# RetNet attention and squared-ReLU FFN on one core: the first block's weight conversion split over three engines, with a third staging buffer and reordered loads

## Chip, cores and metric

One core of a Trainium2 chip runs the whole program. The metric is the device time of one execution in microseconds. The kernel before took 1168.56 us (median of 3 runs, 1168.07 to 1169.2).

## What is computed

The reference, cut to what matters: retention with a decay mask for 8 batches of 8 heads (576 positions, head size 64), and on its output, as 4608 tokens of width 512, two matrix products with a squared ReLU between them (d_ff = 2048). q, k and v are float32; the two weights arrive as float64.

```python
scores = q @ k.T / sqrt(64)                     # per batch and head, 576 x 576
ret = scores * where(rel >= 0, gamma[h] ** rel, 0)
x = (ret @ v).transpose(0, 2, 1, 3).reshape(4608, 512)
h = maximum(x @ w_in, 0.0)                      # w_in 512 x 2048
out = (h * h) @ w_out                           # w_out 2048 x 512
```

## The kernel before

**Attention.** Each batch is cut into chunks of 128 positions (the fifth of a batch has 64), 40 chunks in all. In iteration i of the main loop the kernel runs `retain(i-2)` (L247: the output of a chunk and the running state), `scores(i-1)` (L227) and `turn(i)` (L214: transposes of q and k), and starts the loads of chunk i+2. q, k and v of a full chunk are 256 KB each, loaded by SP's queue at L123. TensorE, VectorE (DVE), ScalarE (ACT), GpSimd (POOL) and SP each work through their own queue in program order. `scores` writes two PSUM banks from the pool `ps_a` (three banks, shared with the transposes and the output of `retain`); VectorE frees them with the masking at L240, which writes `ret`. POOL makes `vs` at L244, from v and the decay `dv`. `qT` is multiplied by the decay `dq` at L223; ScalarE copies kT (L225), the output xT (L272) and the state u (L285). `dq` is 1152 KB and is loaded in one piece behind q, k and v of chunk 0 (L188), `dv` (20 KB) behind it.

**FFN.** Tokens go in 9 blocks of 512. After each of the three parts of an iteration `ffn()` (L474) lets as many steps of the current block run as the tokens done have earned; so TensorE's order of steps is fixed when the program is built. Blocks 1 to 8 use a scheme of seven products (`ffn_in`, `ffn_out`), which needs sums of weight blocks. Block 0 uses the plain products instead: 16 steps `first_in` (L290, eight 128x512 matmuls L297, ReLU on ScalarE L299 into a buffer `r`, square on VectorE L300), then 8 steps `first_out` (L314, sixteen matmuls L322 into four banks `acc`). Beside them the weights are converted and the sums for blocks 1 to 8 are made: `sum_w_in` (L302, four POOL passes per step), and in `first_out` four POOL passes (L328 to L331) over the staging buffer of w_out, after which SP writes its seven parts to DRAM (`w2_dram`, L332, 896 KB). From there blocks 1 to 8 fetch them (L420, 1 MB each).

**Conversion.** The weights are cut into 32 pieces of 512 KB float64 (16 of w_in, then 16 of w_out). `fetch_w` (L146) loads a piece as raw 8-byte words into one of four places in the tiles G that block 0 leaves free. `round_w` (L152) makes float32 of it with five VectorE and two POOL passes of 128x512, in which VectorE waits for POOL in the middle:

```python
nc.vector.tensor_scalar(exp, hi, 20, 0x7FF, ...)                 # L165
nc.gpsimd.tensor_scalar(exp, exp, 1151.0, 896.0, ...)            # L166
nc.gpsimd.tensor_scalar(exp, exp, -896.0, 2.0 ** 23, ...)        # L168
nc.vector.tensor_scalar(bits, hi, 0xFFFFF, 0x100000, ...)        # L170
nc.vector.scalar_tensor_tensor(t, lo, 2.0 ** -32, bits, ...)     # L171
nc.vector.scalar_tensor_tensor(t, t, 2.0 ** -20, exp, ...)       # L172
nc.vector.scalar_tensor_tensor(bits, hi, 0x80000000, bits, ...)  # L173
```

`prepare` (L175) fetches piece j+2 and converts piece j. It is called after each part of every iteration until the 16 pieces of w_in are done (14 of them before the first `first_in`), and then before the steps of block 0. A w_in piece goes straight to `wa` or `wb`; two w_out pieces share a staging buffer `w_stage`, of which there are two (pool `w2_pool`). The results of a block go out through two tiles `o0` and `o1` of `o_pool`.

Of the kernel before, what the change touches and what calls it, by code (L numbers as in the profile page):

```python
# [37 lines left out]
def kernel(  # L38
# [66 lines left out]
    W2_SLOT = {n: j for j, n in enumerate(("B11", "T3", "B21", "B22", "T1", "T2", "T4"))}  # L105
# [4 lines left out]
    exp_room = [G[3][:, 4 + j, :, :].rearrange("p a b -> p (a b)") for j in range(2)]  # L110
# [41 lines left out]
    def round_w(j):  # L152

        t = piece_dst(j)
        if piece_src(j).dtype == F32:
            nc.sync.dma_start(t.rearrange("p (c f) -> p c f", c=N_DM), piece_src(j))
            return  # L160
        words = raw_room[j % 4].bitcast(U32).rearrange("p (n two) -> p n two", two=2)
# [24 lines left out]
    load(0)
    dq = const.tile([128, HP, S], F32, name="dq")
    nc.sync.dma_start(dq, decay_q)  # L188
    dv = const.tile([128, H, NCH], F32, name="dv")
    nc.sync.dma_start(dv, decay_v)  # L190
# [36 lines left out]
    def scores(i):  # L227
# [3 lines left out]
        sc = [ps_a.tile([128, HP, C], F32, tag="a", name=f"sc{e}") for e in range(2)]  # L231
# [82 lines left out]
    def first_out(m):  # L314

        assert 2 * N_M + 2 * m + 1 < n_ready[0]
# [13 lines left out]
        nc.gpsimd.tensor_tensor(t4, b21, t2, op=ALU.subtract)  # L330
        nc.gpsimd.tensor_tensor(b12, b22, b12, op=ALU.subtract)  # L331
        nc.sync.dma_start(w2_dram[:, :, m, :].rearrange("o p d -> p o d"), s[:, 0:7, :])  # L332
        if m == N_M - 1:
            for half in range(2):
                o = o_pool.tile([128, 2, d_model], F32, tag=f"o{half}", name=f"o{half}")
                for j in range(2):
                    (nc.vector.tensor_copy if j else nc.scalar.copy)(o[:, j, :], acc[2 * half + j])
                store(0, half, o)
# [85 lines left out]
    def ffn_out(n, j, tt):  # L424
# [14 lines left out]
        if j == 0:  # L439
            for half in range(2):  # L440
                o_t[half] = o_pool.tile([128, 2, d_model], F32, tag=f"o{half}", name=f"o{half}")
        c11, c12 = o_t[0][:, :, 0:HT], o_t[0][:, :, HT:]
        c21, c22 = o_t[1][:, :, 0:HT], o_t[1][:, :, HT:]
# [113 lines left out]
```

## Time and profile before

| | |
|---|---|
| median of 3 runs | 1168.56 us |
| profiled execution | 1167.34 us |
| its span | 1165.6 us |
| mean granted TensorE clock | 0.971 |
| TensorE busy | 1081.1 us (93%) |
| VectorE, POOL, ScalarE busy | 416.7, 387.3, 146.2 us |
| first matmul of `first_in` | at 66.04 us |
| first matmul of `ffn_in` (block 1) | at 251.10 us |

Times in the rows below are counted from the start of the span. A busy time is the sum of an engine's instructions. The granted clock is that of TensorE as a share of full speed. Behind an arrow stands what ended the idle time before an instruction.

### The profile page before, as it was taken

What the parts mean: (1) busy time and instruction counts of PE and PEld (TensorE: products, weight loads), DVE (VectorE), ACT (ScalarE), POOL (GpSimd) and SP (SyncE); (2) the same over time, 40 slices, a digit from 0 to 9 for tenths busy, and PEclk for the clock granted to TensorE, in tenths of its full rate; (3) what the DMA queues carried; (4) which work ended last, traced back from release to release, by engine and by line L of the source; (5) the groups of instructions that cost most, each with busy time, mean ns of one, the idle gap of its engine ahead of it and who ended that gap; (6) DMA issues with size and microseconds to landing.
All of it is one profiled execution on the core that took longest, in us unless ns stands there. A gap on an engine that the chain in (4) does not pass through costs nothing.

```text
span 1165.6 us, 15121 instructions
## 1 busy us (share of the span) xinstructions
PE 1081.1 (93%) x6464; PEld 881.0 (76%) x6464; DVE 416.7 (36%) x610; ACT 146.2 (13%) x287; POOL 387.3 (33%) x372
## 2 busy tenths in 40 slices
PE   3496987679999999999999999999999999999998
PEld 2353543258888888888888888888888888888886
DVE  4886244544412531243125312431253134302410
ACT  1111200011110111111111111111111011100100
POOL 2443046574502440244024402440244024402520
PEclk9788997789999999999999999999999999999999
DMA  9673043355056114701451146015511550033032
GB/s 257 163 173 91 1 128 128 108 142 153 5 172 190 28 35 134 209 19 29 155 181 37 46 136 195 19 38 162 168 27 55 157 165 1 37 116 138 1 109 109
DMA packets 141571, 122.77 MB, mean 105 GB/s; under 512 B 114496, under 2 KB 129856, under 8 KB 134208
## 3 DMA queue, kind: packets, MB, share of 16 engines
q1 hardware_dynamic: 138912, 112.36, 33.8%
q0 software_dynamic: 2592, 9.44, 2.0%
q8 instruction: 51, 0.84, 0.3%
q14 instruction: 16, 0.13, 0.0%
HBM read 105.01 MB, written 16.78 MB: 104 GB/s over the span
## 4 chain that ended last, share of the span: by engine, by line
PE 79%; POOL 7%; DVE 6%; issue 4%; DMA 3%; SPq 1%; POOLq 0%; DVEq 0%
PE h_b L381 14%; PE o_b L431 13%; PE h_c L381 9%; PE h_a L381 9%; PE o_a L431 9%; PE o_c L431 8%; PE h_ps L297 3%; PE sc L235 3%; PE x_ps L262 3%; PE x_ps L258 2%; DMA w_dram<-w_stage 2%; POOL g L168 2%; POOL g L166 2%; PE acc_ps L322 1%; PE kT_ps L220 1%
## 5 line engine op out<-in xcount | busy, mean ns | idle before, releaser
L431 PE MATMUL o_b<-w,g 128*128 128x256 f32 x768 | 172.5, 381 | 0.0
L431 PEld LDWEIGHTS o_b<-w,g 128*128 128x128 f32 x768 | 144.5, 190 | 19.9
L381 PE MATMUL h_a<-xT,wa 128*128 128x256 f32 x512 | 122.5, 382 | 0.0
L431 PE MATMUL o_c<-w,g 128*128 128x256 f32 x512 | 115.4, 381 | 0.0
L431 PE MATMUL o_a<-w,g 128*128 128x256 f32 x512 | 114.9, 381 | 0.0
L431 PEld LDWEIGHTS o_c<-w,g 128*128 128x128 f32 x512 | 96.2, 190 | 13.6
L431 PEld LDWEIGHTS o_a<-w,g 128*128 128x128 f32 x512 | 96.3, 190 | 13.3
L381 PEld LDWEIGHTS h_a<-xT,wa 128*128 128x128 f32 x512 | 95.8, 190 | 13.7
L322 PE MATMUL acc_ps<-w_stage,g 128*128 128x512 f32 x128 | 67.6, 688 | 30.1 <-DVE w_stage L173 30.1
L408 POOL TENSOR_TENSOR g<-g 128x512 f32<-128x512 f32 x32 | 40.6, 1269 | 118.7 <-DVE g L389 115.4
L322 PEld LDWEIGHTS acc_ps<-w_stage,g 128*128 128x128 f32 x128 | 27.9, 224 | 65.5 <-issue 33.1
L389 DVE SCALAR_TENSOR_TENSOR g<-g 128x512 f32<-128x512 f32 x96 | 75.4, 786 | 3.3
L244 POOL TENSOR_TENSOR vs<-v_ld,dv 128x512 f32<-128x512 f32 (+1 forms) x40 | 42.2, 1055 | 98.8 <-issue 80.6
L400 POOL TENSOR_TENSOR g<-g 128x512 f32<-128x512 f32 x32 | 33.2, 1037 | 119.1 <-ACT g L399 114.7
L342 POOL DMA_DIRECT2D out_dram<-o x18 | 13.5, 748 | 176.7 <-issue 56.1
L240 DVE TENSOR_TENSOR ret<-sc,msk 128x512 f32<-128x512 f32 (+1 forms) x80 | 47.1, 628 | 60.7 <-PE sc L235 60.7
L381 PE MATMUL h_b<-xs,ws 128*128 128x256 f32 x256 | 60.9, 381 | 0.5 <-DVE xs L354 0.5
L381 PE MATMUL h_b<-xT,wb 128*128 128x256 f32 x256 | 60.9, 381 | 0.3 <-POOL xT L355 0.3
L381 PE MATMUL h_c<-xT,ws 128*128 128x256 f32 x256 | 61.0, 381 | 0.0
L381 PE MATMUL h_b<-xs,wb 128*128 128x256 f32 x256 | 61.0, 381 | 0.0
L381 PE MATMUL h_c<-xs,ws 128*128 128x256 f32 x256 | 60.9, 381 | 0.0
L220 PE MATMUL kT_ps<-ident,k_ld 128*128 128x128 f32 (+1 forms) x160 | 25.4, 286 | 36.8 <-DVE ret L240 36.6
(84 smaller groups left out, 1402.1 us busy)
## 6 DMA issues: line engine op xcount, KB each, us to landing
w<-w_dram SPq DMA_DIRECT2D x56, 1024.0 KB, 5.0
out_dram<-o POOLq DMA_DIRECT2D x18, 512.0 KB, 6.0
q_ld<-in_q_dram SPq DMA_DIRECT2D x32, 256.0 KB, 5.9
k_ld<-in_k_dram SPq DMA_DIRECT2D x32, 256.0 KB, 6.5
v_ld<-in_v_dram SPq DMA_DIRECT2D x32, 256.0 KB, 4.3
g<-in_moe_w_in_dram SPq DMA_DIRECT2D x16, 512.0 KB, 4.2
g<-in_moe_w_out_dram SPq DMA_DIRECT2D x16, 512.0 KB, 5.7
w_dram<-w_stage SPq DMA_DIRECT2D x8, 896.0 KB, 4.9
```

What stands on the lines that cost most here:

```text
L220: nc.tensor.transpose(p[:, hp, :cs], loaded[i][j][:cs, 2 * hp:2 * hp + 2, :], ident[:cs, :cs])
L235: nc.tensor.matmul(sc[e][:cs, hp, :cs], lhsT=kT[sl, hp, :cs], rhs=qT[sl, hp, :cs], start=True, stop=True)
L240: nc.vector.tensor_tensor(r[:cs, :, :cs], sc[e][:cs, :, :cs], msk[:cs, :, :cs].to_broadcast([cs, HP, cs]), op=ALU.mult)
L244: nc.gpsimd.tensor_tensor(vs[:cs], loaded[i][2][:cs], dv[:cs, :, ci:ci + 1].to_broadcast([cs, H, D]), op=ALU.mult)
L262: nc.tensor.matmul(p[half, hp, :cs], lhsT=s["vs"][:cs, 2 * hp + e, :], rhs=s["ret"][e][:cs, hp, :cs], start=(ci == 0 and hp == 0), stop=Tr ...
L297: nc.tensor.matmul(p, lhsT=w[:, cc, :], rhs=xT[0][:, cc, :], start=(cc == 0), stop=(cc == N_DM - 1))
L322: nc.tensor.matmul(acc[ts], lhsT=g0(m + e * N_M)[:, ts * 128:(ts + 1) * 128], rhs=s[:, 2 * e:2 * e + 2, :].rearrange("p a b -> p (a b)"), ...
L381: nc.tensor.matmul(p[:, mm, :], lhsT=w[:, c, :], rhs=xs[n][right][:, c, :], start=(j in OPENS and mm == 0 and c == 0), stop=(j in CLOSES a ...
L389: nc.vector.scalar_tensor_tensor(t, t, 0.0, t, op0=ALU.max, op1=ALU.mult)
L400: nc.gpsimd.tensor_tensor(g["A11"], g["A11"], g["A11"], op=ALU.mult)
L408: nc.gpsimd.tensor_tensor(g["S3"], g["A11"], g["S1"], op=ALU.subtract)
L431: nc.tensor.matmul(p[:, tt, :], lhsT=G[m // 2][:, G_SLOT[left], m % 2, tt * 128:(tt + 1) * 128], rhs=w2[j][:, m, :], start=(j in OPENS and ...
```

## The change

The conversion of a piece becomes three functions. `round_a` has two VectorE passes (exponent, mantissa bits) and three new ScalarE passes: the low word scaled to float32 and written back in place, the exponent clamped and shifted by a Relu with a bias, and the sign as +1 or -1 over the high word. `round_b` multiplies exponent and sign on POOL. `round_c` adds the two parts of the mantissa and multiplies by the scale, on VectorE. `prepare` issues `round_a` and `round_b` of piece j and then `round_c` of piece j-1, so the stages of two pieces overlap; after it, piece j+4 is fetched, into one of five places instead of four. The first five pieces are fetched together in iteration 1, behind the loads of chunk 3. `prepare` no longer runs in iterations 0 to 2 but from iteration 3 to 5 (three times each), and then before the steps of block 0 as before, up to two pieces further ahead.

For w_out there are three staging buffers in turn (the third is the tile of `o_pool`, which becomes one tile for both halves of an output block). The four sums are made on VectorE as soon as both pieces are converted (`sum_w_out`), instead of on POOL in `first_out`, and the writes to DRAM (`keep_w_out`, now two DMAs) are issued when the next buffer's first piece is done. The square in `first_in` goes from VectorE to POOL, in place, without the buffer `r`. The scores of chunks 0 to 3 use the banks of `ps_f` instead of `ps_a`. Of `dq`, the first 128 columns are loaded right behind q of chunk 0, `dv` behind k, and the rest behind v.

The diff's core (the order of the parts in `w2_dram`, the assertions and the indexing of `o` are left out):

```diff
-    g_room = [G[2][:, 2 + j:4 + j, :, :] for j in (0, 2)] + [G[3][:, j:j + 2, :, :] for j in (0, 2)]
+    g_room = [G[2][:, 2 + j:4 + j, :, :] for j in (0, 2)] + [G[3][:, j:j + 2, :, :] for j in (0, 2, 4)]
...
+            if i == 0 and name == "q":
+                nc.sync.dma_start(dq[:, :, 0:C], decay_q[:, :, 0:C])
+            if i == 0 and name == "k":
+                nc.sync.dma_start(dv, decay_v)
+        if i == 0:
+            nc.sync.dma_start(dq[:, :, C:], decay_q[:, :, C:])
...
-            stage[m] = w2_pool.tile([128, N_M, d_model // 2], F32, tag="w2", name="w2_stage")
+            pool, tag = (o_pool, "o") if m % 3 == 2 else (w2_pool, "w2")
+            stage[m] = pool.tile([128, 8, d_model // 2], F32, tag=tag, name="w2_stage")
...
+    def round_a(j):
+        t = halves[j] = piece_dst(j)
+        words = raw_room[j % N_RAW].bitcast(U32).rearrange("p (n two) -> p n two", two=2)
+        f32s = raw_room[j % N_RAW].rearrange("p (n two) -> p n two", two=2)
         lo, hi = words[:, :, 0], words[:, :, 1]
-        bits = t.bitcast(U32)
         exp = exp_room[j % 2].bitcast(U32)
         nc.vector.tensor_scalar(exp, hi, 20, 0x7FF, op0=ALU.logical_shift_right, op1=ALU.bitwise_and)
-        nc.gpsimd.tensor_scalar(exp, exp, 1151.0, 896.0, op0=ALU.min, op1=ALU.max)
-        nc.gpsimd.tensor_scalar(exp, exp, -896.0, 2.0 ** 23, op0=ALU.add, op1=ALU.mult)
-        nc.vector.tensor_scalar(bits, hi, 0xFFFFF, 0x100000, op0=ALU.bitwise_and, op1=ALU.bitwise_or)
-        nc.vector.scalar_tensor_tensor(t, lo, 2.0 ** -32, bits, op0=ALU.mult, op1=ALU.add)
-        nc.vector.scalar_tensor_tensor(t, t, 2.0 ** -20, exp.bitcast(F32), op0=ALU.mult, op1=ALU.mult)
-        nc.vector.scalar_tensor_tensor(bits, hi, 0x80000000, bits, op0=ALU.bitwise_and, op1=ALU.bitwise_or)
+        nc.vector.tensor_scalar(t.bitcast(U32), hi, 0xFFFFF, 0x100000, op0=ALU.bitwise_and, op1=ALU.bitwise_or)
+        nc.scalar.activation(f32s[:, :, 0], lo, AF.Copy, scale=2.0 ** -32)
+        nc.scalar.activation(exp, exp, AF.Relu, bias=exp_bias[:, 0:1], scale=2.0 ** 23)
+        nc.scalar.activation(f32s[:, :, 1], hi, AF.Sign, bias=exp_bias[:, 1:2], scale=-1.0)
+    def round_b(j):
...
+        nc.gpsimd.tensor_tensor(exp_room[j % 2], exp_room[j % 2], f32s[:, :, 1], op=ALU.mult)
+    def round_c(j):
...
+        nc.vector.tensor_tensor(t, f32s[:, :, 0], t.bitcast(U32), op=ALU.add)
+        nc.vector.scalar_tensor_tensor(t, t, 2.0 ** -20, exp_room[j % 2], op0=ALU.mult, op1=ALU.mult)
+    def sum_w_out(m):
+        b11, b12, b21, b22, t1, t2, t4, t3 = (stage[m][:, j, :] for j in range(8))
+        nc.vector.tensor_tensor(t1, b12, b11, op=ALU.subtract)
+        nc.vector.tensor_tensor(t3, b22, b12, op=ALU.subtract)
+        nc.vector.tensor_tensor(t2, b22, t1, op=ALU.subtract)
+        nc.vector.tensor_tensor(t4, b21, t2, op=ALU.subtract)
+    def keep_w_out(m):
+        nc.sync.dma_start(w2_dram[0, :, m, :], stage[m][:, 0, :])
+        nc.sync.dma_start(w2_dram[1:7, :, m, :].rearrange("o p d -> p o d"), stage[m][:, 2:8, :])
+    def prepare():
+        j = n_made[0]
...
+                round_a(j)
+                round_b(j)
...
+        j -= 1
+        if j >= 0:
+            if wide:
+                round_c(j)
+                fetch_w(j + N_RAW)
+            wi, m, e = pieces[j]
+            if wi == 1 and m > 0 and e == 0:
+                keep_w_out(m - 1)
+            if wi == 1 and e == 1:
+                sum_w_out(m)
+                if m == N_M - 1:
+                    keep_w_out(m)
...
-        sc = [ps_a.tile([128, HP, C], F32, tag="a", name=f"sc{e}") for e in range(2)]
+        pool, tag = (ps_f, "f") if i < TOK // C else (ps_a, "a")
+        sc = [pool.tile([128, HP, C], F32, tag=tag, name=f"sc{e}") for e in range(2)]
...
-        r = work2.tile([128, TOK], F32, tag="qT", name="r")
+        r = g0(m + e * N_M)
         nc.scalar.activation(r, p, AF.Relu)
-        nc.vector.tensor_tensor(g0(m + e * N_M), r, r, op=ALU.mult)
+        nc.gpsimd.tensor_tensor(r, r, r, op=ALU.mult)
...
-        nc.gpsimd.tensor_tensor(t1, b12, b11, op=ALU.subtract)
-        nc.gpsimd.tensor_tensor(t2, b22, t1, op=ALU.subtract)
-        nc.gpsimd.tensor_tensor(t4, b21, t2, op=ALU.subtract)
-        nc.gpsimd.tensor_tensor(b12, b22, b12, op=ALU.subtract)
-        nc.sync.dma_start(w2_dram[:, :, m, :].rearrange("o p d -> p o d"), s[:, 0:7, :])
...
+                if n_made[0] <= 2 * N_M + 5 + (2 * args[0] if f == first_out else 0):
+                    prepare()
...
+    def early(i):
+        if TOK // C - 1 <= i <= TOK // C + 1:
+            prepare()
...
+        if i + 2 == TOK // C - 1:
+            for j in range(N_RAW):
+                fetch_w(j)
```

## Rows read from the trace of the kernel before

**Rows 1.** Busy us (x instructions) by stretch, then clock, DMA share, GB/s

```profile
0.00:66.04 66.04, 27.91 (x297) 24.10 (x297) 45.18 (x71) 8.90 (x18) 24.70 (x37) 0.84 0.85 207
66.04:112.44 46.40, 36.65 (x164) 18.37 (x161) 36.33 (x57) 6.42 (x13) 16.62 (x20) 0.89 0.49 128
112.44:170.10 57.66, 57.58 (x260) 29.13 (x256) 17.06 (x25) 8.41 (x18) 19.16 (x24) 1.00 0.17 51
170.10:251.10 81.00, 51.01 (x169) 23.30 (x169) 37.65 (x54) 3.54 (x10) 47.13 (x60) 0.79 0.42 120
251.10:1165.60 914.50, 907.91 (x5588) 786.14 (x5584) 280.46 (x405) 118.92 (x232) 279.74 (x232) 1.00 0.33 99
```

**Rows 2.** TensorE's waits: who for whom, us in total, times, longest us

```profile
PE kT_ps L220 <- DVE ret L240: 36.6, 5, 9.6
PE acc_ps L322 <- DVE w_stage L173: 30.1, 5, 7.4
PE sc L235 <- DVE qT L223: 6.3, 3, 4.6
```

**Rows 3.** TensorE's timeline: start us, busy us, instruction, idle before and releaser

```profile
33.84 1.11 PE L220 MATMUL kT_ps<-ident,k_ld 128*128 128x128 f32 x4 [6.83 <-DVE ret L240]
...
47.31 1.12 PE L220 MATMUL kT_ps<-ident,k_ld 128*128 128x128 f32 x4 [6.82 <-DVE ret L240]
...
106.12 4.90 PE L297 MATMUL h_ps<-xT,wb 128*128 128x512 f32 x8
...
152.79 7.13 PE L322 MATMUL acc_ps<-w_stage,g 128*128 128x512 f32 x16
...
174.82 9.90 PE L322 MATMUL acc_ps<-w_stage,g 128*128 128x512 f32 x16 [4.79 <-DVE w_stage L173]
```

**Rows 4.** VectorE's timeline, 170 to 192 us

```profile
173.35 0.69 DVE L172 SCALAR_TENSOR_TENSOR w_stage<-w_stage,g 128x512 f32<-128x512 f32 x1
...
175.47 0.98 DVE L171 SCALAR_TENSOR_TENSOR w_stage<-g,w_stage 128x512 f32<-128x512 uint32 x1
176.96 1.20 DVE L172 SCALAR_TENSOR_TENSOR w_stage<-w_stage,g 128x512 f32<-128x512 f32 x1 [0.51 <-POOL g L168]
...
188.75 0.43 DVE L170 TENSOR_SCALAR w_stage<-g 128x512 uint32<-128x512 uint32 x1 [8.59 <-DMA w_dram<-w_stage]
```

**Rows 5.** POOL's timeline, the same stretch

```profile
175.18 0.72 POOL L166 TENSOR_SCALAR g<-g 128x512 uint32<-128x512 uint32 x1 [6.97 <-DVE g L165]
...
177.69 1.05 POOL L308 TENSOR_TENSOR ws<-ws,wa 128x256 f32<-128x256 f32 x1
...
181.50 0.72 POOL L329 TENSOR_TENSOR w_stage<-w_stage 128x256 f32<-128x256 f32 x1
...
184.49 0.62 POOL L168 TENSOR_SCALAR g<-g 128x512 uint32<-128x512 uint32 x1
```

**Rows 6.** ScalarE by line: busy us, mean ns of one, idle before

```profile
L285 ACT COPY u_sb<-u_ps 64x256 f32<-64x256 f32 x64 | 23.4, 366 | 0.5
L272 ACT COPY xT<-x_ps 128x512 f32<-128x512 f32 (+1 forms) x44 | 22.0, 509 | 176.5 <-PE x_ps L262 176.5
L225 ACT COPY kT<-kT_ps 128x512 f32<-128x512 f32 (+1 forms) x40 | 21.7, 543 | 287.1 <-PE kT_ps L220 287.0
...
L299 ACT ACTIVATE r<-h_ps 128x512 f32<-128x512 f32 x16 | 9.5, 597 | 58.8 <-DVE g L300 26.2 <-PE h_ps L297 24.5 <-PE x_ps L258 8.0
...
L225 ACT ACT_TABLE_LOAD x1 | 1.3, 1283 | 0.8 <-PEq L539 0.8
```

**Rows 7.** All engines' timeline, first 20 us

```profile
4.38 1.08 PE L220 MATMUL qT_ps<-ident,q_ld 128*128 128x128 f32 x4 [4.38 <-DMA q_ld<-in_q_dram]
...
10.26 0.69 DVE L223 TENSOR_TENSOR qT<-qT_ps,dq 128x512 f32<-128x512 f32 x1 [10.26 <-DMA dq<-in_decay_q_dram]
...
15.15 0.43 DVE L165 TENSOR_SCALAR g<-g 128x512 uint32<-128x512 uint32 x1 [4.20 <-DMA g<-in_moe_w_in_dram]
```

**Rows 8.** POOL by line

```profile
L400 POOL TENSOR_TENSOR g<-g 128x512 f32<-128x512 f32 x32 | 33.2, 1037 | 119.1 <-ACT g L399 114.7 <-DMA k_ld<-in_k_dram 4.4
```

More of the change, by code (lines that the diff above doesn't have):

```diff
@@ L104 @@
     G_SLOT = {n: j for j, n in enumerate(("A11", "A12", "A22", "S1", "S2", "S3", "S4"))}
-    W2_SLOT = {n: j for j, n in enumerate(("B11", "T3", "B21", "B22", "T1", "T2", "T4"))}
+    W2_SLOT = {n: j for j, n in enumerate(("B11", "B21", "B22", "T1", "T2", "T4", "T3"))}
     w2_dram = dram.tile([7, 128, N_M, d_model // 2], F32, name="w2_dram")
-    g_room = [G[2][:, 2 + j:4 + j, :, :] for j in (0, 2)] + [G[3][:, j:j + 2, :, :] for j in (0, 2)]
+    g_room = [G[2][:, 2 + j:4 + j, :, :] for j in (0, 2)] + [G[3][:, j:j + 2, :, :] for j in (0, 2, 4)]
     raw_room = [t.rearrange("p a b c -> p (a b c)") for t in g_room]
-    exp_room = [G[3][:, 4 + j, :, :].rearrange("p a b -> p (a b)") for j in range(2)]
+    exp_room = [G[2 + j][:, 6, :, :].rearrange("p a b -> p (a b)") for j in range(2)]
+    N_RAW = len(raw_room)
     def g0(m):
@@ L152, in round_w @@
[L152 to L161, printed above, removed]
+        if j < len(pieces) and piece_src(j).dtype != F32:
+            raw = raw_room[j % N_RAW].bitcast(I64).rearrange("p (c f) -> p c f", c=N_DM)
+            nc.sync.dma_start(raw, piece_src(j))
+    halves = {}
+    def round_a(j):
+        t = halves[j] = piece_dst(j)
+        words = raw_room[j % N_RAW].bitcast(U32).rearrange("p (n two) -> p n two", two=2)
+        f32s = raw_room[j % N_RAW].rearrange("p (n two) -> p n two", two=2)
@@ new lines, in round_c @@
+    def round_c(j):
+        t = halves.pop(j)
+        f32s = raw_room[j % N_RAW].rearrange("p (n two) -> p n two", two=2)
+        nc.vector.tensor_tensor(t, f32s[:, :, 0], t.bitcast(U32), op=ALU.add)
[6 more added lines that the diff above has]
+        nc.vector.tensor_tensor(t4, b21, t2, op=ALU.subtract)
@@ new lines, in keep_w_out @@
+    def keep_w_out(m):
+        nc.sync.dma_start(w2_dram[0, :, m, :], stage[m][:, 0, :])
+        nc.sync.dma_start(w2_dram[1:7, :, m, :].rearrange("o p d -> p o d"), stage[m][:, 2:8, :])
+    n_made = [0]
+    def prepare():
+        j = n_made[0]
+        if j > len(pieces):
+            return
+        n_made[0] += 1
+        wide = piece_src(0).dtype != F32
+        if j < len(pieces):
+            if wide:
+                round_a(j)
+                round_b(j)
+            else:
+                nc.sync.dma_start(piece_dst(j).rearrange("p (c f) -> p c f", c=N_DM), piece_src(j))
+        j -= 1
+        if j >= 0:
+            if wide:
+                round_c(j)
[7 more added lines that the diff above has]
+                    keep_w_out(m)
@@ L186 @@
+    dq = const.tile([128, HP, S], F32, name="dq")
+    dv = const.tile([128, H, NCH], F32, name="dv")
+    exp_bias = const.tile([128, 2], F32, name="exp_bias")
+    nc.gpsimd.memset(exp_bias[:, 0:1], -896.0 * 2.0 ** 23)
+    nc.gpsimd.memset(exp_bias[:, 1:2], 2.0 ** 31)
     load(0)
[L187 to L190, printed above, removed]
     load(1)
-    fetch_w(0)
-    fetch_w(1)
@@ L325, in first_out @@
         sum_w_in(m)
-        b11, b12, b21, b22, t1, t2, t4 = (s[:, j, :] for j in range(7))
-        nc.gpsimd.tensor_tensor(t1, b12, b11, op=ALU.subtract)
-        nc.gpsimd.tensor_tensor(t2, b22, t1, op=ALU.subtract)
-        nc.gpsimd.tensor_tensor(t4, b21, t2, op=ALU.subtract)
-        nc.gpsimd.tensor_tensor(b12, b22, b12, op=ALU.subtract)
-        nc.sync.dma_start(w2_dram[:, :, m, :].rearrange("o p d -> p o d"), s[:, 0:7, :])
-        if m == N_M - 1:
[L334 to L338, printed above, removed]
+        if m == N_M - 1:
+            o = o_pool.tile([128, 2, 2, d_model], F32, tag="o", name="o")
+            for ts in range(N_TS):
+                half, j = divmod(ts, 2)
+                (nc.vector.tensor_copy if j else nc.scalar.copy)(o[:, half, j, :], acc[ts])
+                if j:
+                    store(0, half, o)
     def store(n, half, o):
         row = n * TOK + half * HT
-        nc.gpsimd.dma_start(out[row:row + HT, :].rearrange("(a p) d -> p a d", p=128), o)
+        nc.gpsimd.dma_start(out[row:row + HT, :].rearrange("(a p) d -> p a d", p=128), o[:, half, :, :])
     def sum_x(n):
@@ L370, in ffn_in @@
         if mp == 0 and j == 0:
-            assert n_ready[0] == len(pieces)
+            assert n_made[0] == len(pieces) + 1
             for nxt in range(2):
@@ L439, in ffn_out @@
         if j == 0:
[L440 to L443, printed above, removed]
+            o_t[0] = o_pool.tile([128, 2, 2, d_model], F32, tag="o", name="o")
+        c11, c12 = o_t[0][:, 0, :, 0:HT], o_t[0][:, 0, :, HT:]
+        c21, c22 = o_t[0][:, 1, :, 0:HT], o_t[0][:, 1, :, HT:]
         if j == 0:
@@ L459, in ffn_out @@
             nc.vector.tensor_tensor(c21, p, c21, op=ALU.add)
-            store(n, 1, o_t[1])
+            store(n, 1, o_t[0])
     steps = []
```

24 lines of the change are left out of this document (6 added, 18 removed).

## The prediction, made before the changed kernel was run

> **What bounds the kernel now.** I read the span cut into five stretches first [rows 1], then TensorE's own waits [rows 2], then TensorE's timeline [rows 3], to find which engine sets each stretch. From 251.10 us on, the matmuls of blocks 1 to 8 keep TensorE busy for 907.91 of 914.50 us at a granted clock of 1.00. The change touches nearly nothing there, so what can move lies in the first 251.1 us. There three stretches are bad and one is good: 0 to 66.04 has 27.91 us of matmul, 66.04 to 112.44 loses clock and time, 112.44 to 170.10 is full (57.58 of 57.66 us, clock 1.00), 170.10 to 251.10 has 51.01 of 81.00 us at a mean clock of 0.79. The waits say on whom: 36.6 us on `ret` L240 of VectorE (kT transposes want a score bank back), 30.1 us on `w_stage` L173 (first_out wants converted weights), 6.3 us on `qT` L223 [rows 2]. The timeline puts four of the five `ret` waits into the first stretch, where an iteration takes 13.47 us (33.84 to 47.31), and the five `w_stage` waits into the last [rows 3].
>
> VectorE's timeline shows what stands behind both [rows 4]: a conversion is five passes of 0.43 to 0.69 us alone, and longer beside POOL (L171 0.98, L172 1.20); and L170 of a reused staging buffer waited 8.59 us for the write to `w2_dram`. That write can start only after the four POOL sums of that buffer, so each first_out runs through POOL, a DMA and VectorE before TensorE gets the next weights. POOL's passes are stretched by the same neighbour: L308 took 1.05 us beside VectorE, L329 of the same size 0.72 alone [rows 5].
>
> **Stage A, to the first first_in (66.04 now).** TensorE's order of steps does not change, so I ask when step 1 of block 0 can start. No conversion stands in iterations 0 to 2 any more; eight stand in iterations 3 to 5 ahead of it. The decay's first 128 columns come right behind q, so qT L223 no longer waits to 10.26 us for all 1152 KB [rows 7]; that takes away most of the 6.3 us. After it, loads set the pace. Between q's landing (256 KB, 4.38 us) and piece 0's (3220 KB, 15.15 us) the queue moved 275 KB per us [rows 7]. Ahead of turn(4), which must precede retain(3), now stand four chunks (3072 KB), the decays (1172), five pieces at once (2560) and the half chunk 4 (384): 7188 KB, landed at 4.38 + 6932/275 = 29.6 us. Adding retain(3) and scores(4), some 3.4 us (half of the 13.47 - 6.83 us that an iteration has without its wait [rows 3]), **33 us** is the floor. Piece 0 lands at 4.38 + 4500/275 = 20.7 us. From there ScalarE, in order, does 8 pieces of three passes. No row has ScalarE read 8-byte strides or words; the nearest is its 128x512 Relu, 0.60 us [rows 6], and VectorE reads just these strides at 0.43 (L170) [rows 4], so I take 0.60: 8 x 1.8 = 14.4 us, plus three iterations of kT, xT and two u copies at 1.8 us = 5.4 [rows 6], gives 40.5. VectorE needs 2 x 0.43 + 2 x 0.69 = 2.2 us a piece (it was 2.9 alone), less than that. The multiplication on POOL is like L400, 1.04 us [rows 8], in place of L166 and L168 (0.72 beside VectorE, 0.62 alone [rows 5]). From above: if iterations 3 and 4 still took 13.47 us each, 20.7 + 26.9 = **47**. I take **40**: 26 us gone. The kT wait on `ret` goes since scores 0 to 3 use the four ps_f banks, idle until first_in; next late is the conversion chain on ScalarE and the piece loads.
>
> **Stage B, first_in to the first ffn_in (66.04 to 251.10, 185.1 us).** At full clock and without waits: 57.66 us stand as measured [rows 1]. The steps of the stretch before come to 34.8: 46.40 less the 9.6 us kT wait, less 2 us of cold steps (first_in 4.90 at 106.12, where half of a warm first_out, 7.13 at 152.79, is 3.6 [rows 3]). The last stretch holds five first_out and the attention between them, slow after each wait (9.90 at 174.82 [rows 3]): 51.01 us at a clock of 0.79 are 40.3 at full clock [rows 1]. Sum **132.8**: 52 us less, of which 39.7 are waits and 12.6 the lower clock behind them. That is a pace of some 4.25 us per first_in and 8.0 per first_out, attention included (16 x 4.25 + 8 x 8.0 = 132), which must be fed.
>
> First_in: per step ScalarE has 1.8 + 0.6 + 0.25 (attention) = 2.65 us, VectorE 2.2 + 0.3, POOL 1.04 + 1.04 (the square, moved to it) + 0.15. All below 4.25, with seven finished pieces in hand. The square's departure frees VectorE of 16 passes; the `r` buffer goes, so relu no longer waits on VectorE. First_out: two pieces and four sums of half size on VectorE, 4.4 + 4 x 0.48 + 0.5 (attention's three passes a chunk over 3.7 steps) = 6.8 (a sum has half a pass's size; no row, between 0.35 and 0.69; I take 70%, as POOL's 0.72 is of 1.04); POOL 2 x 1.04 + 4 x 0.72 + 0.3 = 5.3; ScalarE 4.1. All below 8.0. The added wait: L170's successor in a reused buffer waits for first_out(m-1) on TensorE, since its write to DRAM was issued a step earlier. Behind it on VectorE stand the previous piece's two last passes, its sums and `ret`. First_out(m+1) needs only those two passes, some 2.5 us after that wait ends, and TensorE spends 7.0 us in first_out(m) meanwhile: about 4.5 us of slack, so TensorE waits 0.
>
> What may spoil it is VectorE beside POOL. From L166 at 175.18 on, both worked for 4.9 us: five passes of POOL (2 x 0.62 + 3 x 0.72 = 3.4 us alone) and five of VectorE (2 x 0.43 + 3 x 0.69 = 2.9), so 78% of the 6.3 us that they take one by one [rows 4, 5]. By that, first_out has 0.78 x 12.1 = 9.4 us of joint work against 8.0; five steps fall behind by 7 us, of which the slack eats 4.5. From above, if the two engines never worked at once, all 12.1 us would count: 5 x 4.1 - 4.5 = 16 us. I take the rows' 2.5 us (0 to 16). The Trainium skill (SBUF — State Buffer, SBUF: two separate sides) calls the pair of ports that VectorE and GpSimd share an exclusive lock, held for the whole instruction; by it the upper end would be the value. The stretched rows agree in direction, not in full. With 1.5 us more for cold steps at the start, stage B is **137** (132.8 to 150).
>
> **DMA and queues.** From 40 us on, pieces 5 to 20 and five chunks are 12 MB in 68 us, 176 GB/s; the first_out part has 5.8 MB of pieces, 7.3 MB of kept sums and 2 MB of chunks in 64 us, 236 GB/s. The first 66 us ran 207 GB/s at a DMA share of 0.85 and the last stretch 120 at 0.42 [rows 1], so some 245 to 285 GB/s can flow: it fits, tightly, and loads run 5 pieces ahead. SP issues 8 more writes and 1 more decay load; in order, a v load waits for its `vs` and holds later pieces back, covered by that lead. One `o` tile for both halves costs 0 to 1 us at the end (the last sum could wait for the first half's store); I take 0.
>
> **Sum.** Span 40 + 137 + 914.5 = 1091.5. The profiled execution took 1167.34 us for a span of 1165.6, so 1.7 more: 1093.2; the median of the runs is 1.2 above that execution: **1094**, against 1168.56. Own range: 33 + 132.8 + 914.5 + 2.9 = 1083 to 47 + 150 + 915.5 + 2.9 = 1115.
>
> **Rivals.** (1) *ScalarE becomes the bound; slower.* Its three passes are the operation without a row. With a us per piece, 8 pieces in stage A, 14 under first_in and 10 under first_out lose 8(a - 1.8) + 14(a + 0.85 - 4.25) + 5(2a + 0.5 - 8.0) = 32a - 99.5 us. The gain of 74 is eaten at a = 5.4, 1.8 us a pass. At four times the Relu row, 2.4 a pass, the loss is 131: 1225. Against it: VectorE's strided passes are not slow. 0.07.
>
> (2) *A table reload at every Sign and back.* The trace has one load, 1.28 us [rows 6]. Two per piece make a = 4.4, a loss of 41: 1135. For it: Sign is new here. Against it: Copy and Relu alternate now with one load. The Trainium skill (ScalarE: Activation LUTs, Table sets: the hidden batching unit) says tables are loaded as sets, and that cheap functions (it lists relu, copy, identity, abs, not sign) are in every set. By its price of some 2.66 us a switch (What ACT_TABLE_LOAD costs) the estimate would be a = 7.1 and 1222; no row here shows a switch. 0.07.
>
> (3) *VectorE and POOL block each other fully*, or late pieces hold VectorE's queue and `ret` behind them: +8 to +25 us, 1102 to 1119. For it: L172 at 1.20. 0.12.
>
> (4) *The third buffer does not do what it says*: the refill still waits for its DRAM write, and the last stretch stays at 81 us: 1094 + 41 = 1135. Against it: the write now starts at the piece's arrival. 0.04.
>
> **How the numbers follow.** My forecast has 0.70. A measurement can tell about 0.2%, 2.3 us. All but rival 1 end far below: faster 0.93; of rival 1's 0.07, 0.06 slower and 0.01 the same. The range runs from the DMA floor, 1083, to 1120, which takes in rival 3 and leaves out 0.18.
>
> **What would show it.** First first_in at 36 to 44 us; no kT wait on `ret` above 2 us before it; no acc_ps wait above 1 us; granted clock 1.00 from the first first_in on; first ffn_in at 170 to 180 us; the three new ScalarE passes at 0.5 to 0.7 us and one table load. I am wrong if a pass takes over 1 us, if table loads are many, or if the stretch behind the first ffn_in is no longer 914 us.

## The result, and the profile after

The changed kernel takes **1097.98 us** (median of 4 runs, 1095.8 to 1099.91) against 1168.88 us beside it (4 runs): a ratio of 0.9393, 95% interval 0.9373 to 0.9412. The forecast was 1094, range 1083 to 1120. The profiled execution took 1098.46 us with a span of 1096.8, the granted clock 0.992 in the mean (0.971 before). In its code the conversion stands at L170 to L188 (L170 exponent and L172 bits on VectorE; L174, L176, L178 on ScalarE; L182 exponent times sign on POOL; L187, L188 on VectorE), the square at L344, the sums of w_out at L193 to L196.

The span in stretches, cut at the first `first_in`, at 85.97 us, at the first `first_out` and at the first `ffn_in` (columns as in [rows 1]: stretch, length, busy us and count of PE, PEld, DVE, ACT, POOL, granted clock, DMA share, GB/s):

```profile
0.00:43.60 43.60, 27.51 (x296) 23.83 (x296) 24.19 (x36) 20.05 (x35) 14.60 (x22) 0.92 1.00 243
43.60:85.97 42.37, 37.53 (x160) 18.81 (x160) 40.98 (x51) 28.06 (x47) 27.49 (x21) 0.92 0.68 178
85.97:118.27 32.30, 32.30 (x141) 16.20 (x138) 23.54 (x31) 16.47 (x29) 19.09 (x15) 1.00 0.62 178
118.27:183.31 65.04, 65.04 (x289) 32.18 (x287) 54.03 (x74) 25.24 (x42) 43.02 (x42) 1.00 0.56 155
183.31:1096.80 913.49, 907.63 (x5588) 786.13 (x5584) 279.97 (x405) 118.81 (x232) 277.29 (x229) 1.00 0.32 97
```

Against [rows 1] stage A went from 66.04 to 43.60 us (22.4 less), stage B from 185.06 to 139.71 (45.4 less), stage C from 914.50 to 913.49 (1.0 less): together the 68.8 us by which the spans differ. From 85.97 us to the first `ffn_in` TensorE is full at a clock of 1.00; the one loss behind the first `first_in` lies ahead of that. TensorE's waits answer to [rows 2]:

```profile
PE x_ps L306 <- POOL vs L288: 7.3, 2, 4.4
PE qT_ps L263 <- DMA q_ld<-in_q_dram: 5.7, 2, 4.1
PE kT_ps L263 <- DVE ret L284: 4.8, 1, 4.8
```

The 30.1 us on `w_stage` are gone without a rest, and of the 36.6 on `ret` one wait of 4.8 is left. New is POOL's `vs`, 7.3 us. TensorE's timeline shows where these lie:

```profile
28.07 0.44 PE L306 MATMUL x_ps<-ret,vs 128*64 128x128 f32 x4 [2.93 <-POOL vs L288]
...
38.60 0.44 PE L306 MATMUL x_ps<-ret,vs 128*64 128x128 f32 x4 [4.38 <-POOL vs L288]
...
67.58 1.16 PE L279 MATMUL sc<-qT,kT 64*128 64x128 f32 x16
...
77.64 1.12 PE L263 MATMUL kT_ps<-ident,k_ld 128*128 128x128 f32 x4 [4.83 <-DVE ret L284]
78.55 6.00 PE L341 MATMUL h_ps<-xT,wb 128*128 128x512 f32 x8
```

Both `vs` waits are in stage A. The `ret` wait is under `first_in`, and the step behind it took 6.00 us where others take 3.70 (a cold step against a warm one): the granted clock was 0.97 from 60 us to the end of the wait and 0.58 from 77.64 to 84.55, near the lower of its two levels. ScalarE by line, for its new passes:

```profile
L178 ACT ACTIVATE g<-g,exp_bias 128x512 f32<-128x512 uint32 x32 | 24.6, 769 | 7.0 <-DVE wb L172 2.9 <-DVE wa L172 2.0 <-DVE w_stage L172 1.9
...
L176 ACT ACTIVATE g<-g,exp_bias 128x512 uint32<-128x512 uint32 x32 | 23.1, 722 | 55.2 <-DVE g L170 55.2
...
L174 ACT ACTIVATE g<-g 128x512 f32<-128x512 uint32 x32 | 21.6, 676 | 0.1
...
L268 ACT ACT_TABLE_LOAD x1 | 1.3, 1283 | 0.8 <-PEq L585 0.8
```

They take 0.68 to 0.77 us each, with one table load in the whole program, and ScalarE itself waited 55.2 us for L170 of VectorE. So VectorE is to be read next, during `first_in`, and POOL beside it. First VectorE's timeline:

```profile
64.27 0.69 DVE L188 SCALAR_TENSOR_TENSOR wa<-wa,g 128x512 f32<-128x512 f32 x1
64.99 1.40 DVE L170 TENSOR_SCALAR g<-g 128x512 uint32<-128x512 uint32 x1
66.32 1.26 DVE L172 TENSOR_SCALAR wa<-g 128x512 uint32<-128x512 uint32 x1
67.50 0.68 DVE L187 TENSOR_TENSOR wb<-g,wb 128x512 f32<-128x512 f32 x1
68.28 0.69 DVE L188 SCALAR_TENSOR_TENSOR wb<-wb,g 128x512 f32<-128x512 f32 x1
69.00 1.40 DVE L170 TENSOR_SCALAR g<-g 128x512 uint32<-128x512 uint32 x1
...
76.90 0.69 DVE L284 TENSOR_TENSOR ret<-sc,msk 128x512 f32<-128x512 f32 x1
```

and POOL's timeline of the same stretch:

```profile
64.74 1.37 POOL L182 TENSOR_TENSOR g<-g,g 128x512 f32<-128x512 f32 x1 [1.80 <-ACT g L178]
66.07 1.22 POOL L344 TENSOR_TENSOR g<-g 128x512 f32<-128x512 f32 x1
68.52 1.61 POOL L182 TENSOR_TENSOR g<-g,g 128x512 f32<-128x512 f32 x1 [1.23 <-ACT g L178]
70.08 1.22 POOL L344 TENSOR_TENSOR g<-g 128x512 f32<-128x512 f32 x1
```

Read the ends, start plus duration. L182 ends at 66.11, L170 at 66.39; L344 at 67.29, L172 at 67.58; L182 at 70.13, L170 at 70.40: VectorE's pass ends 0.27 to 0.29 us behind POOL's each time, however long it has been open, and alone it takes 0.42 in all. The other way round, L182 at 68.52 started while L188 (to 68.97) was open and took 1.61, while L182 at 64.74 met only 0.22 us of L188 and took 1.37: less the overlap, both are 1.15 to 1.16. The two engines take turns, and a piece costs VectorE 4.01 us (64.99 to 69.00). In rows for the time from piece 0's landing (23.37) to the first `first_in`, and to this `ret`:

```profile
23.37:43.60 20.23, 12.34 (x152) 10.91 (x148) 19.63 (x29) 14.57 (x26) 10.36 (x8) 0.83 1.05 258
23.37:76.90 53.53, 41.55 (x268) 25.17 (x264) 51.79 (x67) 37.16 (x63) 30.60 (x23) 0.93 0.83 210
```

VectorE is open for 19.63 of 20.23 us, where ScalarE is for 14.57, and for 51.79 of 53.53 us. The scores that `ret` reads were done at 68.7 (67.58 + 1.16 in TensorE's timeline); `ret` started at 76.90 only because VectorE's queue was full.

### The profile page after: what moved, and what is told of

It is laid out like the page before. It is cut to its first block, busy times and chain, and to the rows that moved or that the text cites. A ratio compares the mean times of both kernels' runs of the same rounds, so it can differ in the third digit from the quotient of the medians.

```text
span 1096.8 us, 15263 instructions
## 1 busy us (share of the span) xinstructions
PE 1070.0 (98%) x6464; PEld 877.1 (80%) x6464; DVE 422.7 (39%) x594; ACT 208.6 (19%) x383; POOL 381.5 (35%) x326
## 4 chain that ended last, share of the span: by engine, by line
PE 89%; issue 5%; DVE 4%; DMA 1%; SPq 1%; POOLq 0%; POOL 0%; DVEq 0%
PE h_b L419 15%; PE o_b L469 13%; PE h_a L419 10%; PE h_c L419 10%; PE o_a L469 9%; PE o_c L469 9%; PE acc_ps L366 5%; PE h_ps L341 3%; PE sc L279 3%; PE x_ps L306 3%; PE x_ps L302 3%; PE kT_ps L263 1%; PE qT_ps L263 1%; DVE g L170 1%; PE u_ps L323 1%
## 5 line engine op out<-in xcount | busy, mean ns | idle before, releaser
L469 PEld LDWEIGHTS o_c<-w,g 128*128 128x128 f32 x512 | 96.2, 190 | 13.6
L306 PE MATMUL x_ps<-ret,vs 128*64 128x128 f32 (+1 forms) x640 | 59.3, 277 | 7.3 <-POOL vs L288 7.3
L268 ACT COPY kT<-kT_ps 128x512 f32<-128x512 f32 (+1 forms) x40 | 21.7, 542 | 185.8 <-PE kT_ps L263 185.6
L366 PE MATMUL acc_ps<-w_stage,g 128*128 128x512 f32 x128 | 56.6, 596 | 0.0
```

The costliest lines, as they stand in the source:

```text
L306: nc.tensor.matmul(p[half, hp, :cs], lhsT=s["vs"][:cs, 2 * hp + e, :], rhs=s["ret"][e][:cs, hp, :cs], start=(ci == 0 and hp == 0), stop=Tr ...
L366: nc.tensor.matmul(acc[ts], lhsT=g0(m + e * N_M)[:, ts * 128:(ts + 1) * 128], rhs=s[:, 2 * e:2 * e + 2, :].rearrange("p a b -> p (a b)"), ...
L469: nc.tensor.matmul(p[:, tt, :], lhsT=G[m // 2][:, G_SLOT[left], m % 2, tt * 128:(tt + 1) * 128], rhs=w2[j][:, m, :], start=(j in OPENS and ...
```

## The experiments

All are edits of the changed kernel. "Time" is a median of 4 runs, or a single run (marked 1), where 2 us either way is the spread of the changed kernel itself. Stage A is the start of the first `first_in`, stage B runs from there to the first `ffn_in`; both are of the profiled execution. Piece 0 landed at 22.7 to 25.2 us in these traces, so the next column counts stage A from that landing. There the changed kernel and four other versions lie between 20.1 and 20.3 us: what sets these five apart in stage A is the landing, not the edit.

| version | time, us | stage A | from piece 0 | stage B |
|---|---|---|---|---|
| changed kernel | 1097.98 | 43.60 | 20.23 | 139.71 |
| x_mult | 1091.98 | 42.23 | 17.76 | 135.72 |
| u_square | 1098.75 | 42.33 | 19.60 | 140.68 |
| x_vs | 1096.08 | 42.84 | 19.10 | 138.62 |
| b_all | 1091.87 | 42.93 | 17.78 | 134.59 |
| b_mult_square | 1091.48 | 41.73 | 17.74 | 135.92 |
| b_vs_mult | 1093.29 | 41.98 | 17.92 | 136.21 |
| x_act (1) | 1102.0 | 46.79 | 22.69 | 139.74 |
| u_stage (1) | 1118.38 | 51.79 | 26.65 | 150.83 |
| u_two (1) | 1119.27 | 45.20 | 20.25 | 159.16 |
| u_sums (1) | 1129.18 | 44.28 | 20.32 | 167.98 |
| u_scores (1) | 1097.24 | 43.58 | 20.06 | 138.52 |
| u_loads (1) | 1097.69 | 43.27 | 20.20 | 139.28 |

**x_mult: the multiplication of exponent and sign on VectorE.**

```diff
     def round_b(j):
...
-        nc.gpsimd.tensor_tensor(exp_room[j % 2], exp_room[j % 2], f32s[:, :, 1], op=ALU.mult)
...
     def round_c(j):
...
+        nc.vector.tensor_tensor(exp_room[j % 2], exp_room[j % 2], f32s[:, :, 1], op=ALU.mult)
```

> The multiplication of exponent and sign goes from POOL to VectorE (32 passes), all else as changed. By my theory (the two engines exclude each other), 1.4 us of POOL become 0.6 us of VectorE per piece: L170 and L172, 0.86 and 0.8 us in the mean now, fall to near 0.42; POOL has vs at once, so TensorE's 7.3 us wait for vs goes too: first first_in at 38 to 41 us, wait on ret under 3 us, 1088 to 1094. By the rival (VectorE's own load), 32 x 0.6 = 19 us more on the late engine: spacing of conversions 4.5 us, the wait on ret 8 us or more, 1100 to 1108.

1091.98 us (1090.94 to 1092.88), ratio 0.9347 (0.9333 to 0.9361), an interval clear of the changed kernel's. The busiest vector engine got 32 passes more and the kernel became 6 us faster. VectorE's timeline:

```profile
65.31 1.15 DVE L170 TENSOR_SCALAR g<-g 128x512 uint32<-128x512 uint32 x1
66.37 0.42 DVE L172 TENSOR_SCALAR wb<-g 128x512 uint32<-128x512 uint32 x1
66.71 0.69 DVE L187 TENSOR_TENSOR g<-g,g 128x512 f32<-128x512 f32 x1
...
68.76 1.15 DVE L170 TENSOR_SCALAR g<-g 128x512 uint32<-128x512 uint32 x1
```

and the row from piece 0 to the same `ret`:

```profile
24.47:72.09 47.62, 40.41 (x248) 24.14 (x248) 46.86 (x82) 36.68 (x62) 8.82 (x8) 0.93 0.88 228
```

Pieces are 3.45 us apart. Over the same 15 pieces VectorE has 82 instructions where it had 67, in 46.86 us instead of 51.79; POOL's 30.60 us have become 8.82. TensorE's `kT` wait fell from 4.8 to 1.4, stage B by 4.0 us; stage A, though piece 0 landed 1.1 us later, by 1.4, which is 2.5 from the landing on. The time is where the theory had it; the first `first_in` (42.23, expected at 38 to 41) is not: the wait on `vs` went, but 4.7 us of waiting on `ret` came in its place.

**u_square: the square back on VectorE.**

```diff
-        nc.gpsimd.tensor_tensor(r, r, r, op=ALU.mult)
+        nc.vector.tensor_tensor(r, r, r, op=ALU.mult)
```

> The square of first_in goes back from POOL to VectorE (in place), all else as changed. My theory: VectorE and POOL exclude each other, so what counts is the sum of both; a square costs about 0.6 us on VectorE and 1.22 on POOL, so the spacing of conversions under first_in falls from 4.0 to about 3.4 us, and the 4.8 us wait of kT on ret falls to 0 to 2 us: 1091 to 1096. Rival: VectorE's own load is what is late; with 0.6 us more per step the spacing grows to 4.5 and the wait on ret to 8 us or more: 1101 to 1106. The first first_in stays at 43.6 by both.

1098.75 us (1098.13 to 1100.15), ratio 0.9407 (0.9393 to 0.9421): neither expectation. VectorE's timeline has both effects:

```profile
67.75 1.51 DVE L344 TENSOR_TENSOR g<-g 128x512 f32<-128x512 f32 x1 [0.20 <-ACT g L343]
69.19 0.41 DVE L170 TENSOR_SCALAR g<-g 128x512 uint32<-128x512 uint32 x1
69.52 0.41 DVE L172 TENSOR_SCALAR wb<-g 128x512 uint32<-128x512 uint32 x1
```

L170 and L172 are back at 0.41, but the square now waits 0.20 us for its ReLU and meets L182 in their place (1.51, against 0.68 in the versions without L182 on POOL). Pieces are 3.77 us apart, little under 4.01; `ret` started at 76.73 instead of 76.90, and its wait stayed at 4.4.

**x_vs: the conversions of the retain slot moved behind the scores**, so that POOL's `vs` no longer queues behind them.

```diff
             retain(i - 2)
-            early(i)
...
             scores(i - 1)
             early(i)
+            early(i)
```

> The two conversions that stand between retain and scores in iterations 3 to 5 move behind scores, so that POOL makes vs before the multiplications of these pieces. My theory: the 7.3 us that TensorE waits for vs L288 in the changed kernel come from POOL's order, and go to under 2 us; the first first_in starts at 37 to 41 us (43.6 now) and the time falls by 3 to 7 us, to 1091 to 1095. Rival: ScalarE and VectorE hold the same stretch anyway, a wait for ret or for the xT copy takes the place of that for vs, and the first first_in stays within 1.5 us of 43.6, the time within 2 us of 1098.

1096.08 us (1095.24 to 1096.71), ratio 0.938 (0.9364 to 0.9396), which overlaps the changed kernel's interval: some 2 us at most. TensorE's waits show the exchange:

```profile
PE sc L279 <- DVE qT L266: 5.8, 2, 4.2
...
PE x_ps L306 <- POOL vs L288: 0.6, 1, 0.6
```

The wait on `vs` went, 7.3 to 0.6, and one on `qT` came, 5.8: two conversions now stand ahead of `qT` on VectorE. That is the rival's case, by its two signs: the first `first_in` within 1.5 us of 43.6, the time within 2 us of 1098.

**b_all, b_mult_square, b_vs_mult: the edits above together**, all three, the first two, and the first and third.

> All three together: conversions behind scores in iterations 3 to 5, square and multiplication on VectorE; POOL keeps vs and the sums of w_in. By my theory both waits go: first first_in at 36 to 40 us, no kT wait over 1 us, stage B at its 132.8 to 134 us, 1085 to 1090. By the rival (VectorE's load) first_in steps wait for conversions or kT for ret by 10 us or more, and it is slower than the changed kernel, 1100 to 1110.

> Edit: the changed kernel with both the exponent-times-sign multiplication and the square of first_in on VectorE, the conversions where the change has them. Theory (VectorE and POOL take turns, so a POOL pass costs VectorE more than the same pass on VectorE would): pieces under first_in 3.2 us apart as in the version with three edits (it was 4.01 in the changed kernel, 3.45 with the multiplication alone moved), first_in's last step starts its w_out half near 111, the kT wait on ret gone; 1089 to 1092 us. Rival (with POOL out of it, VectorE's own passes delay ret, and the placement of the conversions does the harm in the first stretch): the 4.7 us x_ps wait on ret of the version with the multiplication alone grows, 1093 to 1096 us.

> Edit: the changed kernel with the multiplication on VectorE and the conversions of the retain slot moved behind the scores; the square stays on POOL. Theory (what is left after the multiplication is moved lies in the first stretch, where either placement puts some 5 us of waiting on one of TensorE's steps, and the square on POOL costs VectorE only 0.7 us a piece, which the pace of 3.45 us hides): 1090.5 to 1093 us, the same as with the multiplication alone. Rival (the square's stretching still sets the pace under first_in): 1093 to 1096 us, with a kT wait on ret above 1.5 us.

1091.87 us (1090.77 to 1092.8), 1091.48 (1091.27 to 1092.52) and 1093.29 (1092.32 to 1094.97); ratios 0.9346, 0.9349 and 0.9366 (0.935 to 0.9381). None is told apart from x_mult. b_all missed its 1085 to 1090, b_mult_square came in where it was expected, but with 2.2 us of the `kT` wait left that was to go, and b_vs_mult lies at the line between its two theories, without the `kT` wait on `ret` that the second one named. With nearly all of POOL's work gone, L170 is back at its own length and pieces are 3.2 us apart in b_all and b_mult_square. The mean of L170 from 20 to 185 us follows POOL's passes: 863 ns in the changed kernel, 669 without the square on POOL, 649 without the multiplication there, 486 in b_all. b_all has no wait on `ret` left. What none of x_mult and these three loses is a wait on VectorE in stage A: 4.7 us on `ret` in x_mult and b_mult_square, 4.8 and 5.1 on `qT` in b_all and b_vs_mult. It changes its place with the order of VectorE's queue, and the end stays where it is: 17.7 to 17.9 us behind piece 0's landing in all four.

**x_act: one more ScalarE pass per piece** (a Copy of the sign onto itself).

```diff
         nc.scalar.activation(f32s[:, :, 1], hi, AF.Sign, bias=exp_bias[:, 1:2], scale=-1.0)
+        nc.scalar.activation(f32s[:, :, 1], f32s[:, :, 1], AF.Copy)
```

> One more ScalarE pass per piece (a copy of the sign over itself, 0.65 us, 32 in all); the output is unchanged. My theory: ScalarE is not the bound (it waited 55 us for VectorE's L170); stage B changes by under 2 us, and only stage A, where POOL's vs stands behind ScalarE's passes, gets 1 to 3 us longer: 1098 to 1102. Rival (ScalarE paces the pieces): 24 x 0.65 = 16 us and more, 1112 to 1120.

1102.0 us, the span 3.5 above, the pass 682 ns long. Stage B is the same to 0.03 us (139.74): under `first_in` and `first_out` ScalarE has room for it. Stage A is 3.2 us longer, of which 0.7 is the later landing of piece 0, and POOL's timeline has the way:

```profile
38.20 1.29 POOL L183 TENSOR_TENSOR g<-g 128x512 f32<-128x512 f32 x1 [2.32 <-ACT g L179]
39.44 1.25 POOL L289 TENSOR_TENSOR vs<-v_ld,dv 128x512 f32<-128x512 f32 x1
```

POOL waits for the fourth piece's sign from ScalarE, and `vs` of chunk 3 stands behind that in POOL's queue: 39.44, where the changed kernel has it at 37.21. In stage A ScalarE does set part of the pace.

**u_stage: the three parts of a conversion issued for one piece together.**

```diff
                 round_a(j)
                 round_b(j)
+                round_c(j)
+                fetch_w(j + N_RAW)
...
-            if wide:
-                round_c(j)
-                fetch_w(j + N_RAW)
```

> The three stages of one piece are issued together (round_a, round_b, round_c of piece j), instead of round_c of the piece before; three buffers and all else as changed. My theory: VectorE then waits for ScalarE's three passes and POOL's one within each piece, some 3.5 us, so a piece takes 5.3 to 6 us: first first_in 8 to 16 us later, waits in first_in and first_out, 1140 to 1165. Rival: the queues run ahead enough; a piece stays at 4.0 us and the time within 5 us of 1098.

1118.38 us: 20 us worse, less than expected. TensorE's waits:

```profile
PE x_ps L305 <- DVE ret L283: 12.0, 2, 6.1
PE kT_ps L262 <- DVE ret L283: 11.9, 2, 11.4
...
PE acc_ps L365 <- DVE w_stage L188: 1.4, 2, 0.9
```

VectorE now waits in the middle of each piece (20.4 + 13.6 + 13.5 us for L182, by line, from 20 to 185 us), and `ret` behind it. That costs 8 us in stage A (6.4 from piece 0's landing) and 11 in stage B, but the w_out part, with three buffers, takes even this nearly without a wait (1.4 us).

**u_two and u_sums: the staging of w_out undone in two ways.** u_two uses two staging buffers (`w2_pool` alone, and pieces at most two less far ahead), sums still on arrival; u_sums keeps three buffers, but the four sums return to POOL and, with the write, into `first_out`. First u_two:

```diff
-            pool, tag = (o_pool, "o") if m % 3 == 2 else (w2_pool, "w2")
+            pool, tag = w2_pool, "w2"
```

and u_sums, with the four passes of `sum_w_out` on `nc.gpsimd` and its calls taken out of `prepare`:

```diff
         sum_w_in(m)
+        sum_w_out(m)
+        keep_w_out(m)
```

> Two staging buffers again (conversion two pieces less ahead), sums on VectorE on arrival as changed. My theory: a buffer is refilled only after first_out(m-1) has read it, and two pieces need 9 to 10 us of VectorE and POOL together against 7.0 us of first_out(m): acc_ps waits of 3 to 5 us at five to seven steps, 20 to 35 us with the clock behind them: 1118 to 1133. Rival: making the sums on arrival was all that mattered; waits under 1 us, within 5 us of 1098.

> Three staging buffers stay, but the four sums of w_out go back to POOL in first_out, and the write to DRAM with them. My theory: the acc_ps waits of before came from the chain POOL sums, DRAM write, refill; a third buffer alone only moves it one step away, so waits of 2 to 5 us return at four or five first_out: last part of stage B 10 to 25 us longer, 1108 to 1123. Rival: the third buffer alone covers that chain; no acc_ps wait, within 3 us of 1098.

1119.27 us, as expected, and 1129.18, more than expected. TensorE waits for `w_stage` again, in u_two:

```profile
PE acc_ps L366 <- DVE w_stage L188: 10.8, 4, 4.0
```

and in u_sums:

```profile
PE acc_ps L360 <- DVE w_stage L188: 22.2, 4, 7.5
```

VectorE's timeline of u_sums has the cause, the write that the buffer's next user waits for, as in [rows 4]:

```profile
146.24 0.43 DVE L172 TENSOR_SCALAR w_stage<-g 128x512 uint32<-128x512 uint32 x1 [10.53 <-DMA w_dram<-w_stage]
```

In u_two that wait is 4.4 to 4.5 us (at 141.83 and 154.16). Stage B lost 19.5 and 28.3 us, some 9 and 6 more than the waits on `w_stage`; the steps behind the waits are slow again (9.77 us for a `first_out` at 168.28 in u_two, 7.03 warm). So, by one run each, undoing the early sum and write costs more than undoing the third buffer with its lead, and the wait on `w_stage` is gone only with both. u_sums also moves the sums to another engine; what that alone costs was not tried.

**u_scores and u_loads: the two small parts.** u_scores puts the scores of chunks 0 to 3 back into `ps_a`; u_loads loads `dq` in one piece behind v, and `dv` behind it.

```diff
-        pool, tag = (ps_f, "f") if i < TOK // C else (ps_a, "a")
+        pool, tag = ps_a, "a"
```

and for u_loads, `dv` moved likewise:

```diff
-            if i == 0 and name == "q":
-                nc.sync.dma_start(dq[:, :, 0:C], decay_q[:, :, 0:C])
...
+            nc.sync.dma_start(dq, decay_q)
```

> Edit: the scores of chunks 0 to 3 go back to the ps_a banks. Theory: those banks are then again shared by transposes, scores and outputs, and TensorE waits for VectorE's ret in the first stretch: first first_in about 3 us later (0 to 7), 1098 to 1105 us. Rival (loads and vs set the first stretch, the banks nothing): first first_in within 0.5 us of 43.6, 1097 to 1099 us.

> Edit: dq is again loaded in one piece, behind v of chunk 0, and dv behind it. Theory: the first qT waits again for the 1152 KB, to about 10.3 us, but conversions and vs come later than that, so only 1 to 2 us (0 to 3) of the 4.4 reach the first first_in; 1098 to 1101 us. Rival (the early start is what pulls the first stretch in): all 4.4 us reach it, 1102 to 1103 us.

1097.24 and 1097.69 us: in one run each neither part is worth anything that can be seen. In u_scores three short waits for the banks came (0.19, 1.29 and 2.69 us), but the waits on `vs` shrank from 7.3 to 2.5. In u_loads TensorE's timeline reads:

```profile
10.72 2.08 PE L276 MATMUL sc<-qT,kT 64*128 64x128 f32 x16 [4.17 <-DVE qT L263]
27.76 0.69 PE L303 MATMUL x_ps<-ret,vs 128*64 128x128 f32 x4 [4.74 <-POOL vs L285]
```

The late `dq` costs 4.17 us at the start, and at 27.76 TensorE stands where it stood at 28.07: `vs` of chunk 2 stands in POOL's queue behind the multiplication of piece 0 either way (it starts at 26.46 in u_loads and at 26.78 in the changed kernel, as that multiplication ends).

## Why the prediction was right, point by point

- **Stage A, 40 predicted, 43.60.** The sum was 20.7 for piece 0's landing plus 19.8 of ScalarE's work. Piece 0 landed at 23.37, and 20.2 us followed. So the landing is off by 2.7 us, from a rate of 275 KB per us taken from [rows 7]; the same 4500 KB came at 234 (from 4.12 to 23.37). That the second term fits is luck. Only six pieces, not eight, stand in ScalarE's queue ahead of the `xT` copy that the first `first_in` waited for (the sixth L178 at 42.34, the copy at 42.99), each takes 2.17 us and not 1.8, and ScalarE was open for 14.57 of the 20.23 us. The full engine was VectorE, open for 19.63 (its waits for POOL's turns included), which the prediction put below ScalarE. The path runs from the two through POOL's multiplication to `vs` and `retain`, a queue that the prediction did not look at and in which TensorE lost 7.3 us: from the landing on, the stage is 2.5 us shorter with that pass on VectorE (x_mult) and 2.5 us longer with one more ScalarE pass (x_act). The early `dq` and the `ps_f` banks fall as explanations: undone one at a time, in one run each, they cost nothing that can be seen (both at once was not tried). Of the 22.4 us, staging is worth 6 to 8 (u_stage); how the rest divides between the ScalarE passes, the later start of the conversions and the five early fetches was not tried.
- **First_in, "all below 4.25 us".** This is the step that failed. It held each engine against TensorE's pace by itself: VectorE 2.5 us, POOL 2.23. They take turns, so the two had to be added, to 4.7. Five finished pieces were in hand at 43.60, not seven. A piece took 4.01, which leaves almost nothing to catch up with after a queue that had been full since 23.37 us, and the price was the 4.83 us wait at 77.64 and the cold step of 6.00 behind it. x_mult, which takes a POOL pass away and makes VectorE's list longer, shows it: pieces 3.45 apart and 6 us less. u_square, which takes the other pass away, gains nothing, because the square then waits for POOL's multiplication itself.
- **VectorE beside POOL.** The prediction took 78% of the added times from [rows 4, 5] for joint work. Here the turns are nearly full: the four passes alone take 2.18 us from start to start (0.34 + 0.33 in u_square, 0.78 + 0.73), POOL's two 1.15 and about 1.04 (the one square that fell into the first_out stretch), 4.37 together against 4.01 measured, 92%. By the rule of the Trainium skill (SBUF — State Buffer, SBUF: two separate sides), that the pair is an exclusive lock held for an instruction, the ends above are what one expects; the trace agrees, with L170 at 1.40 instead of 0.42. The 16 us that full turns would have cost in first_out were not paid all the same.
- **First_out, 2.5 us of lost time predicted, none paid.** The estimate of 9.4 us for a pair of pieces was near: L170 of every second piece stood at 134.92, 144.19, 155.06 and 164.66, 9.9 us apart, against 8.1 of TensorE (65.04 / 8). But TensorE waited nowhere in it, so what falls is the 4.5 us of slack: five pieces were finished when it began (L188 of the fifth at 108.84, `first_out` at 118.27), a larger lead. It was nearly used up: for the step at 166.21 the second half of the weights was ready at 169.22, by an estimate half a us before TensorE came to it (half of the step's 7.13 us is over at 169.8). x_mult, with two more VectorE passes per pair there, does wait, 1.6 us.
- **Stage B, 137 predicted, 139.71.** The floor of 132.8 stands: b_all, with no `ret` wait, has 134.59. The rest is 4.8 of wait and 2.3 of cold step. The sign "clock 1.00 from the first first_in" failed (0.92 from 43.60 to 85.97), and so did "first ffn_in at 170 to 180" (183.31).
- **Rivals.** (1) falls: 0.68 to 0.77 us a pass (two of the three above the 0.5 to 0.7 of the signs), and x_act changes stage B by nothing. (2) falls: one load of 1283 ns. (4) falls: no wait on `w_stage`; u_two and u_sums show that the two parts carry it. (3) was right as a mechanism, at a smaller price than its 8 to 25 us: in stage B 4.8 of wait and 2.3 of cold step.
- Stage C is 1.0 us shorter than before; why was not tried. The span is 5.3 us above the sum, and the median lies 0.5 us below the profiled execution instead of 1.2 above, which leaves the 4 us between 1094 and 1098.
- **What stays open.** No version makes the conversion without the three ScalarE passes, so what the split over three engines is worth by itself is not shown. Shown, by one run each, are the overlap of two pieces (u_stage, 20 us), the third buffer with its lead (u_two, 21) and the early sums and writes (u_sums, 31); the three can't be added.

## What to carry to other kernels

Before work goes from a full engine to a neighbour, look in the trace for instructions of the two that stretch side by side. If they take turns, add their times and hold the sum against the pace: here a pass of 0.6 us on a full VectorE was cheaper than one of 1.15 us on a POOL with time to spare, for which VectorE stood still. It need not hold for every pass: the square, moved back alone, met POOL's multiplication there and brought nothing. A staging buffer is free when its last reader is done, so do the late, slow use (a sum, a write to memory) as soon as its data are there. A wait taken out of a stage with several queues returns in the next one (`vs` became `qT`): count the queue behind every moved instruction.

## What the runs showed that had not been expected

VectorE's passes of one strided uint32 input, L170 and L172, wait for a running POOL pass (0.42 to 1.40 us), and POOL's for VectorE's (1.15 to 1.61): a single POOL pass delayed one of these passes by 0.7 to 1.0 us (1.15, 1.26 or 1.40 against 0.42). ScalarE reading 32-bit words at an 8-byte stride takes 676 ns for 128x512, 769 with a bias and the sign, where its contiguous ReLU from PSUM takes 583.
